# Odd-k sequence sums of batches 1 to 7 from rotated rows, in a Fourier mixing plus gated FFN kernel

## The chip, the cores and the metric

The kernel runs on one core of one Trainium2 chip. The metric is the device time of one execution in microseconds (us). The engines are TensorE (PE; its weight loads are listed as PEld), VectorE (DVE), ScalarE (ACT), GpSimd (POOL) and SyncE (SP, which here only issues DMAs).

## What is computed

```python
def _attn_ref(x):                      # x: (8, 3008, 256) float32
    X = np.fft.fft(x, axis=1)
    X = np.fft.fft(X, axis=2)
    return X.real.astype(np.float32)

def _moe_ref(x, w_gate, w_val, w_out): # x: (24064, 256); 256 -> 1536 -> 256
    gate = 1.0 / (1.0 + np.exp(-(x @ w_gate)))
    val = x @ w_val
    return (gate * val @ w_out).astype(np.float32)
```

The second function gets the first one's output, reshaped to 24064 rows. Everything is float32.

## The kernel before

**Names of size.** S = 3008 rows a batch, M = S/2 = 1504, D = 256. By symmetry only the frequencies k = 0 to 1504 of the sequence axis are summed; of these the code treats even and odd k apart, and of each only k up to 752, NE = 377 even and NO = 376 odd ones. The rest follow by adding and subtracting two sums, `ev` and `od` (rows with even and with odd s), in `places` (L443): one DVE sum goes up from k = 0, one comes down from k = M.

**Sequence stage.** Each batch has one. For batches 1 to 7 it stands in `whole` (L450), which runs four groups in this order: odd k with cosines (into tile pk), odd k with sines (into qk), even k with cosines, even k with sines. A group is 12 matmuls (`both` inside `half`, L426): six row slots q, times the two partition halves of 64 rows, which hold the rows of even and of odd s and sum into ev and od. For even k, rows s and 752-s have already been folded into each other (L381), so that each matmul moves only 188 or 189 of the 377 columns; for odd k each matmul moves all 376. Cosine groups sum in PSUM banks po0 and po1, sine groups in po2 and po3. `then` (L437) copies ev to SBUF with ACT, and `places` sums it with od on DVE.

**The rows** of a batch are first copied inside DRAM into a mirrored layout (`mirror_x`, L170), loaded as one tile `x4`, and folded by 24 GpSimd operations (`fold_ops`, L347) that are spread over many steps before the stage: rows s with S-s (L354), these with M-s (L367), then feature d with 256-d (`feat`, L360 to L364), first for odd k, then, after L383 has folded 752-s into s, for even k, in three pieces of two slots each. L362 and L364 write those pieces.

**Tables.** Cosines and sines are held in one tile `st` (ST[0]). Batch 0 uses them in the layout of 126 partitions. For the other batches they are copied in DRAM into a mirrored layout `tr` (`mirror_tables`, L192, nine DMAs on SP at steps 22 to 30) and loaded again over the old ones (`table_again`, L195, four DMAs at step 42).

**Joint E.** Feature column 128 of the batches 1 to 7 is transformed for all of them at once in `e_sums` (L476), at step 40, in the PSUM bank of tag po0; its results go through `places` to a DRAM row `ed`.

**The rest of the time** goes to the gated FFN, in 576 steps i (8 batches x 6 chunks of 252 columns x 12 blocks of 128 of the 1536 hidden features). Weights with the feature transform merged in (G1, G2) and a seed from E give pf = G1·pk (`front_a`) and then pf += G2·qk (`front_b`), with the copy `ae` of the first part taken between them (`part`, L548), so that ae and pf give the two mirrored halves. `gate_a` and `gate_b` (L560 to L591) make the sigmoids on ACT and the products h on DVE. GpSimd forms sums of h blocks (sf, L590). `back` (L597) multiplies h and sf blocks with sums of w_out blocks (wf) in 15 products, five a step, into the banks po0 to po4. It stands five steps behind, so that group p (three steps) is multiplied at steps 3p+5 to 3p+7. After the fourth group of a chunk, the banks are copied to `c` (L614), and `finish` combines them with DVE sums (L637), two or three a step, transposes and stores them.

**Order.** It is written out by hand: every engine executes in the order in which the loop at the end of the kernel (L792 to L814) issues. In step i that is front_a(i), gate_a(i-1), part(i), the seeds of step i+1, gate_b(i-1), five products of `back`, front_b(i), some sums of `finish`, then the side work of this step, put there by `at`. Side work that matters here: e_sums at step 40, table_again at 42, the sequence stage of batch b+1 at step g0 (64 for batch 1, then 112, 184, 256, 328, 400, 472), and the folding of its rows in the 16 or 24 steps before g0 whose number mod 12 is below 4. The next batch's rows are loaded (`load_x`) at g0+1.

[...]

Of the kernel before, what the change touches and what calls it, by code (L numbers as in the profile page):

```python
# [7 lines left out]
F32 = mybir.dt.float32  # L8
# [40 lines left out]
NQ = 6  # L49
# [28 lines left out]
def kernel(  # L78
# [49 lines left out]
    def mm(o, l, r, start, stop):  # L128
        nc.tensor.matmul(o, l, r, start=start, stop=stop, skip_group_check=True)  # L129
# [14 lines left out]
            else:  # L144
                nc.sync.dma_start(out=X[b][0:NP, h : h + 2], in_=xf[b, :, h : h + 2])

    def mirrored(dst, src, full):


        copy = nc.sync.dma_start  # L150
        h, n = dst.shape[1], dst.shape[3] - full
        ops = [lambda: copy(out=dst[HP - 2 : HP, :, NQ - 1, full:],
                            in_=zero[:, :, 0:n].to_broadcast([2, h, n]))]

        def rows(par):
            copy(out=dst[par * HP : (par + 1) * HP, :, 0:N3], in_=src[0:HP, :, par:NQ:2])

        def mirror(par, q):
            t = M // 2 - 2 * q - par
            lo, p0, n = par * HP, t // NQ, HP - 2 * ((par, q) == (0, N3 - 1))  # L160
            copy(out=dst[lo : lo + n, :, N3 + q, full:].rearrange("p h d -> h p d"),
                 in_=src[p0 - n + 1 : p0 + 1, :, t % NQ, full:].rearrange("p h d -> h p d")[:, ::-1])
# [5 lines left out]
    XR = {}  # L168

    def mirror_x(b):  # L170
        XR[b] = dram.tile([P, 4, NQ, D], F32, name=f"xr{b}")
        return mirrored(XR[b], xf[b], 0)
# [6 lines left out]
    ge = const.tile([P, 2, NFT], F32, name="ge")  # L179

    x8 = const.tile([NP, B - 1, 4, NQ], F32, name="x8")
    nil = op.tile([2, 1, NO], F32, name="nil", tag="os")
    zero = dram.tile([2, 1, NO], F32, name="zero")
    table = const.tile([2, 1], F32, name="table")
    tr = dram.tile([P, 2, NQ, NE + NO], F32, name="tr")
# [6 lines left out]
    def mirror_tables():  # L192
        return mirrored(tr, stab, NE)

    def table_again():  # L195

        ST[0] = const.tile([P, 2, NQ, NE + NO], F32, name="st", tag="st")
        for t in range(2):
            nc.sync.dma_start(out=ST[0][:, t, 0:N3], in_=tr[:, t, 0:N3])
            nc.sync.dma_start(out=ST[0][:, t, N3:, NE:], in_=tr[:, t, N3:, NE:])  # L200

# [143 lines left out]
    def fold_ops(b, nq):  # L347
# [12 lines left out]
        def feat(e, v, r, q):  # L360
            e.memset(r[:, q, 0:1], 0.0)
            e.tensor_tensor(r[:, q, 1:HD], v[:, q, 1:HD], v[:, q, D - 1 : HD : -1],  # L362
                            op=ALU.subtract)
            e.tensor_tensor(v[:, q, 1:HD], v[:, q, 1:HD], v[:, q, D - 1 : HD : -1], op=ALU.add)  # L364

        def across(e, blk, q):
            e.tensor_tensor(x4[:, 1 - blk, q], x4[:, 0, q], x4[:, 2, q],  # L367
                            op=(ALU.add, ALU.subtract)[blk])

        parts = [(x4[:, 1], x4[:, 3]), (x4[:, 0], x4[:, 2])]  # L370
        qs = [slice(q, q + nq) for q in range(0, NQ, nq)]
        pool = nc.gpsimd
        if b:

            for i in (0, 2):
                ops += [lambda i=i, q=q: point(pool, i, i + 1, q) for q in qs]
# [9 lines left out]
            parts[0] = x4[:, 3], x4[:, 1]  # L386
            ops += [lambda q=q: feat(pool, *parts[0], q) for q in qs]
# [25 lines left out]

    PQE = {}

    def half(w, d, blk, sn, other=None):


        c0, n = ((0, NE), (NE, NO))[blk]
        ev, od = [bank(name, other and other[i])[:, 0:n] for i, name in enumerate(("ev", "od"))]  # L420

        def sums(*qs):
            for q in sorted(qs, key=lambda q: q % 2):
                mm((ev, od)[q % 2], w(q), ST[0][0:NP, int(sn), q, c0 : c0 + n], q < 2, q >= NQ - 2)

        def both():  # L426

            for r in range(2 - blk):
                for q in range(N3 if blk == 0 else NQ):
                    for par, sum_ in enumerate((ev, od)):  # L430
                        rows = slice(par * HP, par * HP + HP - 1 - (par and q % N3 == N3 - 1))
                        ks = slice(None) if blk else slice(r, n, 2)
                        wq = q if blk else q + N3 * (r ^ int(sn))
                        mm(sum_[:, ks], w(wq)[rows], ST[0][rows, int(sn), q, c0 : c0 + n][:, ks],
                           q == 0 and r == 0, q == (NQ if blk else N3) - 1)

        def then():  # L437
            a = evp.tile([P, NE], F32, name="a", tag="a")[:, 0:n]
            nc.scalar.copy(a, ev)
            return lambda: places(d, blk, sn, a, od)  # L440
        return sums, then, both
# [18 lines left out]
            nc.vector.memset(t[:, NK:], 0.0)  # L460

    def seq_group(b, blk, what, other=None):
        return half(lambda q: W[b, blk][what][:, q, :], PQE[b][what], blk, what == 1, other)


    def e_load(b):
# [9 lines left out]
    def e_sums():  # L476


        ps = bank("pe", 0)
        m = B - 1  # L480
        at_ = lambda blk, par: slice((2 * blk + par) * TB, (2 * blk + par) * TB + m)
        for q in range(0, NQ, 2):
# [7 lines left out]
        a = evp.tile([P, NE], F32, name="a", tag="a")[0:m]  # L490
        e1 = evp.tile([P, NE], F32, name="a", tag="a")[0:m]
        nc.scalar.copy(a, ps[at_(0, 1), 0:NE])
        nc.scalar.copy(e1[:, 0:NO], ps[at_(1, 0), 0:NO])

# [245 lines left out]
    def at(i, *fs):  # L740
        side.setdefault(i, []).extend(fs)
# [129 lines left out]
```

## Time and profile before

| what | value |
|---|---|
| median of 3 runs | 1974.01 us (1973.17 to 1975.24) |
| the profiled execution | 1973.76 us |
| its span, first to last instruction | 1972.0 us |
| mean granted clock of TensorE in it | 0.995 |
| DMA over the span | 101.41 MB, 51 GB/s |

The costliest groups, as the profile lists them (busy us in all, mean of one record):

| line, engine, tile | records | busy us | mean ns |
|---|---|---|---|
| L129 PE pf<-qk and pf<-pk, 252 or 246 columns | 4608 | 1165.8 | 375 |
| L129 PE po<-sf and po<-h, 168 or 164 columns | 5760 | 1007.3 | 305 |
| L129 PE ev (all forms; od runs beside it) | 372 | 98.0 | 414 |
| L590 POOL sf, first two groups | 2112 | 1206.0 | 590 |
| L532 ACT seeds pf<-ek,ge | 1128 | 531.4 | 471 |
| L637 DVE sums c<-c | 949 | 484.3 | 541 |

How to read it: the matmuls are issued through one helper, so all have line L129 and are told apart by the tiles written and read. A float32 matmul of the program leaves two matmul records and two weight-load records. A record lasts longer than the distance to the next one, since matmuls are pipelined; their cost is the distance from start to start. In rows in order of time the first number is the start in us from the start of the span, the second the duration; a bracket at the end gives idle time before the instruction and the instruction that ended it.

### The profile page before, as it was taken

The numbers are of one execution on the slowest core, as the hardware profiler recorded it, in microseconds if no ns is written. First come the engines' busy times: TensorE is split into PE (matmuls) and PEld (weight loads), VectorE is DVE, ScalarE is ACT, GpSimd is POOL, SyncE is SP. The second block draws the span as 40 slices with busy tenths as digits, with TensorE's granted clock in tenths as the row PEclk, the third lists the DMA queues.
The fourth block names the chain that finished last, engine by engine and source line by source line (L and its number), as shares of the span: only waits on it lengthen the run. The fifth ranks groups of instructions, "written<-read, shape, count | busy, mean of one in ns | idle before, by whom it ended". The sixth has DMA issues, their size and how long they took to land.

```text
span 1972.0 us, 34403 instructions
## 1 busy us (share of the span) xinstructions
PE 1935.8 (98%) x11252; PEld 1792.4 (91%) x11252; DVE 1511.7 (77%) x3170; ACT 1339.5 (68%) x3108; POOL 1625.0 (82%) x2843
## 2 busy tenths in 40 slices
PE   6999999999999999999999999999999999999997
PEld 4889889999999899998999989999899999999997
DVE  6888778886787677786778867787678776777777
ACT  3567657766777577775777757777577766777775
POOL 3779888997889788996889868998688996777776
PEclk9999999999999999999999999999999999999999
DMA  8363412212022121212012021211210110011011
GB/s 271 86 134 94 138 52 85 51 22 78 14 51 54 17 76 17 72 31 78 14 28 78 14 78 25 47 48 24 78 19 14 21 20 14 14 20 22 14 19 27
DMA packets 171584, 101.41 MB, mean 51 GB/s; under 512 B 133904, under 2 KB 163218, under 8 KB 168602
## 3 DMA queue, kind: packets, MB, share of 16 engines
q1 hardware_dynamic: 169434, 98.64, 20.6%
q8 instruction: 90, 1.47, 0.3%
q10 hardware_dynamic: 1940, 0.56, 0.1%
q14 instruction: 88, 0.72, 0.1%
q0 software_dynamic: 32, 0.00, 0.0%
HBM read 74.45 MB, written 50.18 MB: 63 GB/s over the span
## 4 chain that ended last, share of the span: by engine, by line
PE 95%; DMA 2%; DVE 2%; ACT 1%; issue 0%; POOL 0%; SPq 0%; ACTq 0%; DVEq 0%; POOLq 0%
PE pf L129 49%; PE po L129 41%; PE ev L129 4%; DMA st<-in_stab_dram 1%; PE ps L129 1%; DMA ge<-G 1%; PE od L129 0%; DMA raw<-in_moe_w_val_dram 0%; DMA xr<-in_xf_dram 0%; DVE c L637 0%; DVE ae L551 0%; DVE wf L337 0%; DVE wx L273 0%; ACT z L585 0%; DVE wx L275 0%
## 5 line engine op out<-in xcount | busy, mean ns | idle before, releaser
L590 POOL TENSOR_TENSOR sf<-h 128x168 f32<-128x168 f32 (+1 forms) x960 | 548.8, 590 | 221.6 <-DVE h L586 221.6
L590 POOL TENSOR_TENSOR sf<-h,sf 128x168 f32<-128x168 f32 (+1 forms) x1152 | 657.2, 590 | 60.5 <-DVE h L586 60.5
L129 PE MATMUL pf<-qk,G 128*128 128x252 f32 (+1 forms) x2304 | 582.4, 375 | 3.1 <-DVE ae L551 2.0
L129 PE MATMUL pf<-pk,G 128*128 128x252 f32 (+1 forms) x2304 | 583.4, 376 | 0.0
L586 DVE TENSOR_TENSOR h<-z 128x252 f32<-128x252 f32 (+1 forms) x576 | 299.1, 519 | 356.9 <-ACT z L585 356.6
L532 ACT ACTIVATE pf<-ek,ge 128x252 f32<-128x252 f32 (+1 forms) x1128 | 531.4, 471 | 18.4
L129 PE MATMUL po<-sf,wf 128*128 128x168 f32 (+1 forms) x3072 | 530.1, 305 | 0.0
L548 ACT ACTIVATE ae<-pf 128x504 f32<-128x504 f32 (+1 forms) x569 | 335.0, 589 | 245.6 <-PE pf L129 245.5
L637 DVE TENSOR_TENSOR c<-c 128x168 f32<-128x168 f32 (+1 forms) x949 | 484.3, 541 | 5.5 <-ACT c L614 0.3
L129 PEld LDWEIGHTS pf<-pk,G 128*128 128x128 f32 x2304 | 436.7, 190 | 52.6 <-issue 2.3
L129 PEld LDWEIGHTS po<-sf,wf 128*128 128x128 f32 x3072 | 472.8, 190 | 8.3
L129 PE MATMUL po<-h,wf 128*128 128x168 f32 (+1 forms) x2688 | 477.2, 306 | 1.7 <-ACT a L497 1.6
L129 PEld LDWEIGHTS po<-h,wf 128*128 128x128 f32 x2688 | 428.8, 191 | 19.0 <-ACT a L497 2.0
L129 PEld LDWEIGHTS pf<-qk,G 128*128 128x128 f32 x2304 | 410.2, 190 | 29.2 <-DVE ae L551 2.6
L572 DVE TENSOR_TENSOR z<-ae,pf 128x504 f32<-128x504 f32 (+1 forms) x569 | 377.4, 663 | 21.5 <-ACT h L567 20.9
L567 ACT ACTIVATE h<-pf 128x252 f32<-128x252 f32 (+1 forms) x576 | 217.9, 378 | 164.0 <-PE pf L129 152.9
L585 ACT ACTIVATE z<-z 128x252 f32<-128x252 f32 (+1 forms) x576 | 231.1, 401 | 80.3 <-DVE z L572 60.1
L584 DVE TENSOR_TENSOR h<-h,pf 128x252 f32<-128x252 f32 (+1 forms) x576 | 231.9, 403 | 0.0
L590 POOL TENSOR_TENSOR sf<-sf 128x168 f32<-128x168 f32 (+1 forms) x192 | 111.3, 580 | 15.1
L590 POOL TENSOR_TENSOR sf<-sf,h 128x168 f32<-128x168 f32 (+1 forms) x192 | 106.6, 555 | 0.0
L129 PE MATMUL ev<-st,x 63*128 63x376 f32 (+4 forms) x372 | 98.0, 414 | 8.3 <-DVE x L364 7.8
L129 PEld LDWEIGHTS ev<-st,x 63*128 63x128 f32 (+1 forms) x372 | 66.4, 187 | 36.1 <-DVE x L364 8.2
(120 smaller groups left out, 861.9 us busy)
## 6 DMA issues: line engine op xcount, KB each, us to landing
x<-xr SPq DMA_DIRECT2D x14, 1536.0 KB
out_dram<-os SPq DMA_DIRECT2D x380, 56.0 KB
xr<-in_xf_dram SPq DMA_DIRECT2D x14, 768.0 KB
xr<-in_xf_dram SPq DMA_DIRECT2D x35, 256.0 KB
ek<-ed SPq DMA_DIRECT2D x39, 126.0 KB
out_dram<-os SPq DMA_DIRECT2D x288, 7.0 KB
st<-in_stab_dram SPq DMA_DIRECT2D x4, 1111.9 KB
x<-in_xf_dram SPq DMA_DIRECT2D x2, 1512.0 KB
```

What stands on the lines that cost most here:

```text
L129: nc.tensor.matmul(o, l, r, start=start, stop=stop, skip_group_check=True)
L532: nc.scalar.activation(PF[i][:, g], EK[i // NFT], AF.Copy, scale=ge[:, g, f : f + 1])
L548: nc.scalar.activation(AP[i], PF[i], AF.Copy, scale=2.0)
L567: nc.scalar.activation(H[p][:, fh, 0:n], PF[i][:, 0], AF.Sigmoid)
L572: nc.vector.tensor_tensor(z[:, :, ::-1], AP.pop(i), PF[i], op=ALU.subtract)
L584: nc.vector.tensor_tensor(h[:, fh, 0:n], h[:, fh, 0:n], PF.pop(i)[:, 1], op=ALU.mult)
L585: nc.scalar.activation(z[:, 0], z[:, 0], AF.Sigmoid)
L586: nc.vector.tensor_tensor(h[:, fh, n:], z[:, 0], z[:, 1], op=ALU.mult)
L590: nc.gpsimd.tensor_tensor(block(p, dst), block(p, a), block(p, b), op=(ALU.subtract, ALU.add)[op])
L637: engine.tensor_tensor(t[:, dst * R : (dst + 1) * R], *v, op=(ALU.subtract, ALU.add)[op])
```

## The change

- **Rotation.** Let t be the angle 2·pi·s/S of a row s. For odd k = 4j+1 and 4j-1, cos(kt) = cos t · (cos 4jt -+ tan t · sin 4jt), and likewise for sines. Six new DVE operations a batch (`turn`) add to each odd-k row slot the tangent times its partner (cosine rows of slot s with sine rows of slot 752-s, and so on) and write the result into the upper feature columns of the same slots, which the folding has left free. They are issued in the last four steps before g0: two, one, two and one.
- **Half tables.** A table j4 of 189 columns (cos t · cos 4jt and cos t · sin 4jt) replaces the 376 odd columns. `table_odd`, once at step 46, makes it from the odd columns that were loaded: two GpSimd sums of 3x187 columns, each followed by an ACT multiply by 0.5, six tiny GpSimd operations at the edges, and three DVE operations on three columns for the tangents.
- **Odd-k groups.** Still 12 matmuls a group, each of 189 columns: slots 0 to 2 sum into the first 189 columns of ev and od, slots 3 to 5 into the next 189.
- **Emptying of odd-k groups.** For ev and for od, one ACT copy of the first 189 columns to SBUF and two DVE operations of 188 columns (sum for k = 4j+1, difference for 4j-1) into a scratch part of the table tile; then `places` as before, but from that scratch. Before, it was one ACT copy of 376 columns and `places`.
- **Tables.** The mirrored copy `tr` in DRAM goes, with its nine DMAs. `table_again` loads only three slots a half, with four DMAs of 64 partitions, straight from the input; the tile is divided into the tables, j4, the scratch and the tangents.
- **Joint E.** `e_sums` takes the PSUM bank of tag po4 instead of po0.
- Batch 0 and the even-k groups keep their work.

```diff
     def table_again():
-        ST[0] = const.tile([P, 2, NQ, NE + NO], F32, name="st", tag="st")
+        full = const.tile([P, 2 * NQ * (NE + NO)], F32, name="st", tag="st")
+        sizes = (2 * N3 * (NE + NO), 2 * N3 * NJ, 2 * NO, N3, N3)
...
         for t in range(2):
-            nc.sync.dma_start(out=ST[0][:, t, 0:N3], in_=tr[:, t, 0:N3])
-            nc.sync.dma_start(out=ST[0][:, t, N3:, NE:], in_=tr[:, t, N3:, NE:])
+            for par in range(2):
+                nc.sync.dma_start(out=ST[0][par * HP : (par + 1) * HP, t], in_=stab[0:HP, t, par:NQ:2])
+
+    def table_odd():
+        odd, j4 = ST[0][:, :, :, NE:], ST[1]
+        for t in range(2):
+            nc.gpsimd.tensor_tensor(j4[:, t, :, 1 : NJ - 1], odd[:, t, :, 2::2], odd[:, t, :, 1 : NO - 1 : 2],
+                                    op=ALU.add)
+            nc.scalar.mul(j4[:, t, :, 1 : NJ - 1], j4[:, t, :, 1 : NJ - 1], 0.5)
...
+        nc.vector.reciprocal(ST[4], odd[:, 0, :, 0])
+        nc.vector.tensor_tensor(ST[3], odd[:, 1, :, 0], ST[4], op=ALU.mult)
+        nc.vector.tensor_scalar(out=ST[4], in0=ST[3], scalar1=-1.0, scalar2=None, op0=ALU.mult)
...
+            slots = x4.rearrange("p i q d -> p (i q) d")
+            def turn(q, minus):
+                y = [slots[:, q : q + 16 : 15], slots[:, q + N3 : q + N3 + 10 : 9]]
+                if minus:
+                    y.reverse()
+                nc.vector.scalar_tensor_tensor(
+                    out=y[0][:, :, HD:D], in0=y[1][:, :, 0:HD], scalar=(ST[3], ST[4])[minus][:, q : q + 1],
+                    in1=y[0][:, :, 0:HD], op0=ALU.mult, op1=ALU.add)
...
+                        if blk:
+                            out_, wq = sum_[:, r * NJ : (r + 1) * NJ], q + N3 * r
+                            tab = ST[1][rows, r ^ int(sn), q]
...
         def then():
+            a = evp.tile([P, 2 * NJ], F32, name="a", tag="a")
+            if b and blk:
+                for par, sum_ in enumerate((ev, od)):
+                    f = a[:, par * NJ : (par + 1) * NJ]
+                    nc.scalar.copy(f, sum_[:, 0:NJ])
+                    for r, op_ in enumerate((ALU.add, ALU.subtract)):
+                        nc.vector.tensor_tensor(ST[2][:, par, r::2], f[:, r : NJ - 1 + r],
+                                                sum_[:, NJ + r : 2 * NJ - 1 + r], op=op_)
+                return lambda: places(d, blk, sn, ST[2][:, 0], ST[2][:, 1])
...
     def e_sums():
-        ps = bank("pe", 0)
+        ps = bank("pe", NB - 1)
...
-    for i, f in enumerate(mirror_tables()):
-        at(2 * i0 - 2 + i, f)
     at(3 * i0, e_fold)
     at(3 * i0 + 4, lambda: e_sums()())
     at(3 * i0 + 6, table_again)
+    at(3 * i0 + 10, table_odd)
...
+            for i, f in enumerate(TURN.pop(b + 1)):
+                at(slots[-4 + i * 4 // 6], f)
```

More of the change, by code (lines that the diff above doesn't have):

```diff
@@ L106 @@
     N3 = NQ // 2
+    NJ = NO // 2 + 1
     assert D == 256 and M % 4 == 0 and NP * NQ > M // 2 and NQ % 2 == 0
@@ L145, in load_x, with mirror_x @@
                 nc.sync.dma_start(out=X[b][0:NP, h : h + 2], in_=xf[b, :, h : h + 2])
-    def mirrored(dst, src, full):
+    XR = {}
+    def mirror_x(b):
         copy = nc.sync.dma_start
-        h, n = dst.shape[1], dst.shape[3] - full
-        ops = [lambda: copy(out=dst[HP - 2 : HP, :, NQ - 1, full:],
-                            in_=zero[:, :, 0:n].to_broadcast([2, h, n]))]
+        src = xf[b]
+        dst = XR[b] = dram.tile([P, 4, NQ, D], F32, name=f"xr{b}")
+        ops = [lambda: copy(out=dst[HP - 2 : HP, :, NQ - 1],
+                            in_=zero[:, :, 0:D].to_broadcast([2, 4, D]))]
         def rows(par):
@@ L160, in mirror @@
             lo, p0, n = par * HP, t // NQ, HP - 2 * ((par, q) == (0, N3 - 1))
-            copy(out=dst[lo : lo + n, :, N3 + q, full:].rearrange("p h d -> h p d"),
-                 in_=src[p0 - n + 1 : p0 + 1, :, t % NQ, full:].rearrange("p h d -> h p d")[:, ::-1])
+            copy(out=dst[lo : lo + n, :, N3 + q].rearrange("p h d -> h p d"),
+                 in_=src[p0 - n + 1 : p0 + 1, :, t % NQ].rearrange("p h d -> h p d")[:, ::-1])
         for par in range(2):
@@ L166, in mirrored @@
         return ops
[L168 to L172, printed above, removed]
     dt = const.tile([P, 2, D], F32, name="dt")
@@ L181 @@
     x8 = const.tile([NP, B - 1, 4, NQ], F32, name="x8")
-    nil = op.tile([2, 1, NO], F32, name="nil", tag="os")
-    zero = dram.tile([2, 1, NO], F32, name="zero")
+    nil = op.tile([2, 1, D], F32, name="nil", tag="os")
+    zero = dram.tile([2, 1, D], F32, name="zero")
     table = const.tile([2, 1], F32, name="table")
-    tr = dram.tile([P, 2, NQ, NE + NO], F32, name="tr")
     ed = dram.tile([B, NK + 1], F32, name="ed")
@@ L190, in load_table @@
             yield nc.sync.dma_start(out=ST[0][0:NP, t, q : q + nq], in_=stab[:, t, q : q + nq])
-    def mirror_tables():
-        return mirrored(tr, stab, NE)
     def table_again():
-        ST[0] = const.tile([P, 2, NQ, NE + NO], F32, name="st", tag="st")
-        for t in range(2):
-            nc.sync.dma_start(out=ST[0][:, t, 0:N3], in_=tr[:, t, 0:N3])
-            nc.sync.dma_start(out=ST[0][:, t, N3:, NE:], in_=tr[:, t, N3:, NE:])
+        full = const.tile([P, 2 * NQ * (NE + NO)], F32, name="st", tag="st")
+        sizes = (2 * N3 * (NE + NO), 2 * N3 * NJ, 2 * NO, N3, N3)
+        at_ = [sum(sizes[0:i]) for i in range(6)]
+        st, jt, eo, *tans = [full[:, at_[i] : at_[i + 1]] for i in range(5)]
+        ST[:] = [st.rearrange("p (t q k) -> p t q k", t=2, q=N3),
+                 jt.rearrange("p (t q k) -> p t q k", t=2, q=N3),
+                 eo.rearrange("p (h k) -> p h k", h=2), *tans]
+        for t in range(2):
+            for par in range(2):
[6 more added lines that the diff above has]
+            nc.scalar.mul(j4[:, t, :, 1 : NJ - 1], j4[:, t, :, 1 : NJ - 1], 0.5)
+        nc.gpsimd.tensor_copy(j4[:, 0, :, 0:1], odd[:, 0, :, 0:1])
+        nc.gpsimd.memset(j4[:, 1, :, 0:1], 0.0)
+        for par in range(2):
+            rows = slice(par * HP, (par + 1) * HP)
+            nc.gpsimd.tensor_copy(j4[rows, par, :, NJ - 1 :], odd[rows, par, :, NO - 1 :])
+            nc.gpsimd.memset(j4[rows, 1 - par, :, NJ - 1 :], 0.0)
+        nc.vector.reciprocal(ST[4], odd[:, 0, :, 0])
+        nc.vector.tensor_tensor(ST[3], odd[:, 1, :, 0], ST[4], op=ALU.mult)
+        nc.vector.tensor_scalar(out=ST[4], in0=ST[3], scalar1=-1.0, scalar2=None, op0=ALU.mult)
     assert NPR == 6
@@ L345 @@
     W = {}
+    TURN = {}
     def fold_ops(b, nq):
@@ L386, in fold_ops @@
             parts[0] = x4[:, 3], x4[:, 1]
+            slots = x4.rearrange("p i q d -> p (i q) d")
[6 more added lines that the diff above has]
+                    in1=y[0][:, :, 0:HD], op0=ALU.mult, op1=ALU.add)
+            TURN[b] = [lambda q=q, minus=minus: turn(q, minus) for q in range(N3) for minus in range(2)]
             ops += [lambda q=q: feat(pool, *parts[0], q) for q in qs]
@@ L408, in fold_ops @@
         for blk, (v, r) in enumerate(parts):
+            if b and blk:
+                W[b, blk] = v[:, :, HD:D], r[:, :, HD:D]
+                continue
             W[b, blk] = (v[:, :, 0:HD], r[:, :, 0:HD],
@@ L414, with half @@
     PQE = {}
-    def half(w, d, blk, sn, other=None):
-        c0, n = ((0, NE), (NE, NO))[blk]
+    def half(b, w, d, blk, sn, other=None):
+        c0, n = ((0, NE), (NE, 2 * NJ if b else NO))[blk]
         ev, od = [bank(name, other and other[i])[:, 0:n] for i, name in enumerate(("ev", "od"))]
@@ L426, in both @@
         def both():
-            for r in range(2 - blk):
-                for q in range(N3 if blk == 0 else NQ):
+            for r in range(2):
+                for q in range(N3):
                     for par, sum_ in enumerate((ev, od)):
[L431 to L435, printed above, removed]
-        def then():
-            a = evp.tile([P, NE], F32, name="a", tag="a")[:, 0:n]
+                        rows = slice(par * HP, par * HP + HP - 1 - (par and q == N3 - 1))
+                        if blk:
+                            out_, wq = sum_[:, r * NJ : (r + 1) * NJ], q + N3 * r
+                            tab = ST[1][rows, r ^ int(sn), q]
+                        else:
+                            out_, wq = sum_[:, r::2], q + N3 * (r ^ int(sn))
+                            tab = ST[0][rows, int(sn), q, r:NE:2]
+                        mm(out_, w(wq)[rows], tab, q == 0 and r == 0, q == N3 - 1)
+        def then():
+            a = evp.tile([P, 2 * NJ], F32, name="a", tag="a")
+            if b and blk:
+                for par, sum_ in enumerate((ev, od)):
[5 more added lines that the diff above has]
+                return lambda: places(d, blk, sn, ST[2][:, 0], ST[2][:, 1])
+            a = a[:, 0:n]
             nc.scalar.copy(a, ev)
@@ L462, in seq_group @@
     def seq_group(b, blk, what, other=None):
-        return half(lambda q: W[b, blk][what][:, q, :], PQE[b][what], blk, what == 1, other)
+        return half(b, lambda q: W[b, blk][what][:, q, :], PQE[b][what], blk, what == 1, other)
     def e_load(b):
@@ L489, in e_sums @@
         nc.vector.memset(er[:, NK:], 0.0)
-        a = evp.tile([P, NE], F32, name="a", tag="a")[0:m]
-        e1 = evp.tile([P, NE], F32, name="a", tag="a")[0:m]
+        a = evp.tile([P, 2 * NJ], F32, name="a", tag="a")[0:m, 0:NE]
+        e1 = evp.tile([P, 2 * NJ], F32, name="a", tag="a")[0:m, 0:NE]
         nc.scalar.copy(a, ps[at_(0, 1), 0:NE])
```

## Prediction

> **What bounds the kernel now.** I read the page's busy table and chain first, then TensorE's rows in order of time, then the engines that feed the seven sequence stages.
>
> ```profile
> span 1972.0 us, 34403 instructions
> ...
> PE 1935.8 (98%) x11252; PEld 1792.4 (91%) x11252; DVE 1511.7 (77%) x3170; ACT 1339.5 (68%) x3108; POOL 1625.0 (82%) x2843
> ...
> PE 95%; DMA 2%; DVE 2%; ACT 1%; issue 0%; POOL 0%; SPq 0%; ACTq 0%; DVEq 0%; POOLq 0%
> ```
>
> PE is busy for 98% of the span and is 95% of the chain, so time taken off PE's queue comes off the end, as long as no other engine takes its place. The change works in the seven sequence stages. This is PE in the last of them:
>
> ```profile
> 1620.71 1.01 PE L129 MATMUL pf<-qk,G 128*128 128x252 f32 x4
> 1621.66 0.58 PE L129 MATMUL ev<-st,x 63*128 63x376 f32 x1
> 1621.66 0.58 PE L129 MATMUL od<-st,x 63*128 63x376 f32 x1
> ...
> 1629.03 0.47 PE L129 MATMUL ev<-st,x 63*128 63x376 f32 x1
> 1629.05 0.47 PE L129 MATMUL od<-st,x 62*128 62x376 f32 x1
> 1629.35 0.33 PE L129 MATMUL ev<-st,x 63*128 63x189 f32 x1
> 1629.37 0.33 PE L129 MATMUL od<-st,x 63*128 63x189 f32 x1
> 1629.51 0.33 PE L129 MATMUL ev<-st,x 63*128 63x189 f32 x1
> ...
> 1633.50 1.12 PE L129 MATMUL pf<-pk,G 128*128 128x252 f32 x4
> ```
>
> An ev and an od matmul start within 0.02 us of each other: the two halves of the partitions run side by side, so the pair is the unit. Each matmul leaves two records. The odd-k part (376 columns) goes from 1621.66 to 1629.35, 24 pairs 0.318 us apart; the even-k part (189 or 188 columns) has 24 pairs 0.168 us apart; the stage takes 11.84 us. All seven do, at 279.22, 440.86, 677.02, 913.18, 1149.34, 1385.50 and 1621.66. T below is the time since a stage's start.
>
> **Matmuls.** The odd-k part keeps 24 pairs and their weight loads, but each moves 189 columns. The even-k row has this very shape, 63x189 with loads of 63x128, at 0.168 us. So a stage loses 24 x (0.318 - 0.168) = 3.6 us, seven lose **25.2 us**. The bounds are 0 (0.318 stays) and 3.7 (its output is no longer strided).
>
> **Product banks.** Odd k with cosines uses banks 0 and 1, with sines 2 and 3, and the even-k groups take the same banks again. The second use now comes 4.0 us after the first instead of 7.6. The old emptying in the same stage:
>
> ```profile
> 1622.51 1.16 DVE L637 TENSOR_TENSOR c<-c 128x168 f32<-128x168 f32 x2
> 1626.25 0.55 DVE L444 TENSOR_TENSOR pk<-a,od 128x376 f32<-128x376 f32 x1 [2.58 <-ACT a L439]
> 1626.72 0.54 DVE L447 TENSOR_TENSOR pk<-a,od 128x376 f32<-128x376 f32 x1
> ```
>
> That is one ACT copy (0.47) and two DVE sums. The new one is two ACT copies and four DVE sums of 188, then the two old placing sums, which no longer hold a bank. Per column, L584 (252 columns from PSUM, 0.40) and L572 (504, 0.66) give about 1.03 ns over 0.15 us; 188 columns cost 0.34 and a copy of 189 0.33. Odd cosines end on PE at T 2.3; the ACT copy to 2.65; DVE, free since T 2.0, leaves bank 0 at 3.3 and bank 1 at 3.8; placing to 4.75. PE wants them at T 4.13: no wait. Sines: done at 4.3, DVE from 4.75, banks 2 and 3 free at 5.3 and 5.85; PE wants them at 6.15. The margins are 0.3 us, and placing sums that read only SBUF can stretch while POOL runs: L586 takes 0.42 alone and 0.61 beside POOL. Two such sums stand ahead of banks 2 and 3, so I charge **0.3 us** a stage in the five stages of batches 3 to 7 (bounds 0 and 1.5), 1.5 us in all. DVE ends some 1.8 us behind PE's last pair, as before.
>
> [...] If DVE bound the stage throughout, it would last 2.66 + 2 x 2.44 + 2 x 1.09 = 9.7 us instead of 8.24 and the kernel some 1962 us.
>
> **POOL is late in two stages.** The even-k group also needs folded rows from POOL, in three pieces of two row slots. Its fifth matmul needs the last, now at T 4.13 + 4 x 0.336 = 5.47 (before: 9.1). The last piece in batch 2 and in batch 7:
>
> ```profile
> 447.93 0.72 POOL L364 TENSOR_TENSOR x<-x 128x254 f32<-128x254 f32 x1
> ...
> 1624.90 0.72 POOL L364 TENSOR_TENSOR x<-x 128x254 f32<-128x254 f32 x1
> ```
>
> They end at T 7.79 and 3.96; batch 1's at 6.57; batches 3 to 6 as 7. POOL has no gap ahead of them, so what slows it arrives here. The new DVE work beside it (six turns, then placing sums) slows POOL by about 0.14 each (L362: 0.72 alone, 0.86 beside DVE); I take 0.6 in all (0 to 1.5). Then PE stands 6.57 + 0.6 - 5.47 = **1.7 us** in batch 1, **2.9 us** in batch 2, nothing in the others. PE is in order, so everything queues behind this wait.
>
> [...]
>
> **Turns.** Six DVE instructions of 2x128 columns a batch, all SBUF: L586 (252 columns) bounds each between 0.42 and its longest, 1.56; its median is 0.47; I take 0.55. They wait for row pieces that POOL finished some ten iterations earlier. Two, one, two, one of them fall into the stage's last four iterations; behind them wait DVE's L572, then ACT's second sigmoid, then DVE's L586. In these iterations DVE stands idle about 1.1 us for that sigmoid; 3.3 us of turns go into about 4.4. Cost 0; without that cover 3.3 us a batch.
>
> **Tables, once.** The nine mirroring DMAs go (SP alone issues them; PE has no gap there): 0. The four reloads move 2259 KB instead of 3387 KB, are issued at about 201 and should land by 212, when DMA share has fallen to 0.41. Their readers come at about 223.8:
>
> ```profile
> 222.40 0.40 ACT L585 ACTIVATE z<-z 128x252 f32<-128x252 f32 x1
> 223.28 0.38 ACT L567 ACTIVATE h<-pf 128x252 f32<-128x252 f32 x1 [0.48 <-PE pf L129]
> 224.13 0.59 ACT L548 ACTIVATE ae<-pf 128x504 f32<-128x504 f32 x1 [0.47 <-PE pf L129]
> ```
>
> Here `table_odd` puts two ACT multiplies behind z, each waiting for a POOL sum of 561 columns. POOL's sums of group 14 end at 223.8 (L590: 223.24 + 0.60). By L367 (512 columns, 1.27) and L383 (384, 1.00) such a sum takes 1.4 us; so they end at 225.2 and 226.7 and the second multiply (0.65) at 227.4. h, ae and the seeds queue behind it: ae comes at 227.7 instead of 224.13, and PE's front_b, which started at 225.35, at 228.25. That costs **2.9 us** (2.5 with sums of 1.2; 5.7 if the stride doubles them). POOL runs 2.2 us late after it, which three iterations of distance to the products cover. DVE's three tiny operations (each between L460's 0.06 and 0.5) sit in that same halt.
>
> **Joint E.** PE's wait of 1.62 us for bank 0 at 203.73 goes. But front_b then still waits for ae at 206.48, whose chain (two copies, DVE's er sums, ACT) does not depend on the bank: gain 0. Bank 4 is emptied by ACT at 199.07, while PE wants it at 198.98: 0.2 lost.
>
> **Sum**: 25.2 - 1.5 - 1.7 - 2.9 - 2.9 - 0.2 = 16.0. The profiled execution took 1973.76 (1.76 outside its span), so 1957.8; the median of the runs is 0.25 higher: **1958.0 us**.
>
> **Rivals.**
> 1. Nothing waits: POOL keeps ahead and ACT's halt is covered. For it: nearly 3.6 us a stage are cleared in five of seven anyway. Against: T 6.57 and 7.79. 25.2 off, or 22.3 with the halt: 1949 to 1951.5. Chance 0.13.
> 2. Emptying or POOL's lateness binds in every stage: DVE's SBUF sums take the 0.7 to 0.9 of the er sums at 203.71. Then a stage keeps 1.0 to 2.1 us instead of 3.3: about 1966, up to 1970. Against: POOL is nearly through in five stages. Chance 0.15.
> 3. The pairs do not get closer than 0.318, weight loads (0.185 each) holding them: 1974 to 1977. Against: the even-k row. Chance 0.05.
> 4. Slower: the turns. If each takes over (4.4 + 3.6) / 6 = 1.33 us, they outgrow DVE's idle time and the stage's gain together; at L586's longest, 1.56, a batch loses 1.3 us net, seven 9, plus ACT's halt: 1986. Against: a median of 0.47. Chance 0.07.
>
> **Numbers.** The forecast, 1953 to 1963, has 0.60. 1950 to 1967 takes in most of rivals 1 and 2 and the bounds above, and leaves out about 0.2. Faster by over 0.2% (about what a measurement here can tell from no change; below 1970) comes to 0.13 + 0.60 + 0.15 = 0.88, within 0.2% to 0.05, slower to 0.07.
>
> **What would show it.** Odd-k pairs of 63x189 at 0.168 us; stages of about 8.5 us for batches 3 to 7, 10 for batch 1 and 11 for batch 2, where PE waits for POOL's L364; one PE gap of about 3 us near 225, ending on ae; no PE wait for DVE's turns. Wrong: waits of PE for bank sums over 1 us a stage, POOL's last pieces later than T 5.5 in batches 3 to 7, or PE gaps in the four iterations ahead of a stage.

## The result, and the profile after

The changed kernel takes 1966.14 us (median of 5 runs, 1965.11 to 1974.25) and the kernel before 1974.01 (5 runs, 1971.70 to 1978.11): ratio 0.9965, 95% interval 0.9942 to 0.9989. On a second chip the ratio was 0.9952 (0.9938 to 0.9965). So it is faster by 0.35 to 0.5%: 7.9 us where the forecast had 16.0. The profiled execution took 1966.45 us with a span of 1964.6, 7.4 us shorter than before; the rest of this text accounts for these 7.4 against 16.0. The lines of `mm` and others have moved: L134 was L129, L388 was L364, L598 was L548, L640 was L590, L386 was L362; L418 is `turn`, L483 and L485 the new emptying, L494 and L497 `places`, L211 and L213 `table_odd`.

From the page: span, busy time and shares of the chain.

```profile
span 1964.6 us, 34539 instructions
...
PE 1920.6 (98%) x11252; PEld 1791.5 (91%) x11252; DVE 1567.0 (80%) x3271; ACT 1341.0 (68%) x3124; POOL 1639.9 (83%) x2851
...
PE 90%; DVE 5%; POOL 3%; ACT 1%; DMA 1%; issue 0%; SPq 0%; DVEq 0%; ACTq 0%; POOLq 0%
```

PE is still the bound, but DVE and POOL now stand on the chain with 8% together, where they had 2%. TensorE's rows in the last stage:

```profile
1616.99 0.42 PE L134 MATMUL ev<-st,x 63*128 63x189 f32 x1
1617.00 0.42 PE L134 MATMUL od<-st,x 63*128 63x189 f32 x1
1617.26 0.32 PE L134 MATMUL ev<-st,x 63*128 63x189 f32 x1
1617.26 0.32 PE L134 MATMUL od<-st,x 63*128 63x189 f32 x1
1617.41 0.32 PE L134 MATMUL ev<-st,x 63*128 63x189 f32 x1
...
1620.95 0.33 PE L134 MATMUL ev<-st,x 63*128 63x189 f32 x1
```

The 24 odd-k pairs now stand 0.16 us apart, and the odd-k part lasts from 1616.99 to 1620.95, 3.96 us instead of 7.69. Without any wait a stage would take 11.84 - 24 x (0.318 - 0.160) = 8.05 us. The seven stages took 11.01, 12.63 and five times 9.17. Three places lost the difference, and two more lost time outside the stages.

**Stages of batches 3 to 7: 1.12 us each.** VectorE in the last stage, then two rows each of TensorE and GpSimd beside it:

```profile
1619.57 0.61 DVE L485 TENSOR_TENSOR st<-a,ev 128x188 f32<-128x188 f32 x2 [0.60 <-ACT a L483]
1620.10 0.60 DVE L485 TENSOR_TENSOR st<-a,od 128x188 f32<-128x188 f32 x2
1620.73 0.88 DVE L494 TENSOR_TENSOR pk<-st 128x376 f32<-128x376 f32 x1
1621.53 1.07 DVE L497 TENSOR_TENSOR pk<-st 128x376 f32<-128x376 f32 x1
1622.70 0.61 DVE L485 TENSOR_TENSOR st<-a,ev 128x188 f32<-128x188 f32 x2
1623.23 0.60 DVE L485 TENSOR_TENSOR st<-a,od 128x188 f32<-128x188 f32 x2
1623.87 0.55 DVE L494 TENSOR_TENSOR qk<-st 128x376 f32<-128x376 f32 x1
1624.34 0.54 DVE L497 TENSOR_TENSOR qk<-st 128x376 f32<-128x376 f32 x1
```

```profile
1623.46 0.57 PE L134 MATMUL ev<-st,x 63*128 63x189 f32 x2 [0.27 <-DVE st L485]
1623.98 0.40 PE L134 MATMUL od<-st,x 63*128 63x189 f32 x1
```

```profile
1620.48 0.72 POOL L386 TENSOR_TENSOR x<-x 128x254 f32<-128x254 f32 x1
1621.28 0.91 POOL L388 TENSOR_TENSOR x<-x 128x254 f32<-128x254 f32 x1
```

Banks 2 and 3 come free when the second pair of L485 rows is through, at 1623.3 and 1623.8. PE wanted bank 2 at 1623.0 and began at 1623.46, and its od half still later, at 1623.98. In front of those rows stand the two placing sums of pk, 0.88 and 1.07 us; the same sums into qk take 0.55 and 0.54. The difference is GpSimd, which runs L386 and L388 until 1622.2. The rows show how each engine held up the other: L494 ends 0.41 us after L386, L497 ends 0.41 us after L388, and L388, begun while L494 ran, takes 0.91 us instead of 0.72. So it goes in the whole trace: 18 placing sums from `st` began beside a GpSimd instruction, and each ends 0.40 to 0.42 us after that one's end, whatever its length (0.71 to 1.07 us); the 10 that met none take 0.54 to 0.55. The L485 sums, which read one input from PSUM, are not held up: the 44 that began beside GpSimd take 0.33 to 0.35 each. Nor were the placing sums of the kernel before, which read `od` from PSUM: nine began beside GpSimd and took 0.54 to 0.55. The change gave the placing sums two inputs in SBUF, and with them this wait.

**Stages of batches 1 and 2: 2.96 and 4.58 us.** TensorE in batch 1, then in batch 2:

```profile
288.96 0.32 PE L134 MATMUL od<-st,x 63*128 63x188 f32 x1
291.89 0.43 PE L134 MATMUL ev<-st,x 63*128 63x188 f32 x1 [2.61 <-POOL x L388]
...
292.34 0.33 PE L134 MATMUL ev<-st,x 63*128 63x188 f32 x1
...
292.51 0.33 PE L134 MATMUL ev<-st,x 63*128 63x188 f32 x1
```

```profile
454.23 0.68 PE L134 MATMUL ev<-st,x 63*128 63x188 f32 x1 [2.63 <-POOL x L388]
...
455.02 0.52 PE L134 MATMUL ev<-st,x 63*128 63x188 f32 x1
...
455.33 0.52 PE L134 MATMUL ev<-st,x 63*128 63x188 f32 x1
...
457.94 0.32 PE L134 MATMUL ev<-st,x 63*128 63x188 f32 x1
```

Both wait 2.6 us for POOL's last piece of rows. But behind the second wait the pairs stand 0.31 us apart instead of 0.17 until 457.5: the granted clock is at half there (0.50), for 3.41 us from 454.26, and that makes 1.6 us more.

**The halt at step 46: 4.13 us.** TensorE, then ScalarE:

```profile
227.57 1.12 PE L134 MATMUL pf<-qk,G 128*128 128x252 f32 x4 [2.16 <-ACT ae L598]
228.53 1.48 PE L134 MATMUL pf<-pk,G 128*128 128x252 f32 x4
229.80 0.77 PE L134 MATMUL po<-h,wf 128*128 128x168 f32 x2
```

```profile
224.94 0.67 ACT L213 ACTIVATE st<-st 128x561 f32<-128x561 f32 x1 [2.24 <-POOL st L211]
226.10 0.67 ACT L213 ACTIVATE st<-st 128x561 f32<-128x561 f32 x1 [0.49 <-POOL st L211]
226.68 0.36 ACT L617 ACTIVATE h<-pf 128x252 f32<-128x252 f32 x1
226.94 0.58 ACT L598 ACTIVATE ae<-pf 128x504 f32<-128x504 f32 x1
```

The multiplies wait for GpSimd's sums and ae queues behind them; the wait is 2.16 us, and once more the clock is halved for 3.41 us behind it, from 228.98. Matched one by one with their rows before the change, TensorE's rows come 4.13 us later behind the halt than ahead of it.

**Turns: 2.0 us.** Busy time in the 12.40 us ahead of the stages of batches 1, 2, 3 and 7 in the kernel before (a row's pairs are PE, PEld, DVE, ACT, POOL):

```profile
266.80:279.20 12.40, 12.40 (x73) 11.58 (x71) 8.86 (x20) 9.74 (x23) 12.24 (x22) 1.00 0.31 49
428.40:440.80 12.40, 12.40 (x73) 11.46 (x71) 9.56 (x22) 10.12 (x24) 12.32 (x22) 1.00 0.32 53
664.60:677.00 12.40, 12.40 (x72) 11.42 (x71) 7.42 (x20) 9.86 (x23) 12.02 (x23) 1.00 0.29 44
1609.20:1621.60 12.40, 12.40 (x73) 11.46 (x71) 7.40 (x20) 9.81 (x23) 11.98 (x23) 1.00 0.24 42
```

DVE had 5.0 us idle ahead of batches 3 and 7, but 3.5 and 2.8 ahead of batches 1 and 2. The 42 turns took 0.785 us in the mean (0.65 to 1.04), so six take 4.7. From the end of stage 1 to the start of stage 2 went 149.79 us before and 151.28 after, with waits of PE for ae of 0.20 and 0.39 in it; 0.54 was lost ahead of stage 1. Between the later stages it is 224.3 us in both.

The joint E's two waits, 1.62 and 1.05, became one of 2.87 at 206.37; TensorE's rows behind it stand 0.1 us earlier than before.

### The profile page after: what moved, and what is told of

It reads as the page before. It is cut to its first block, busy times and chain, and to the rows that moved or that the text cites. A ratio compares the mean times of both kernels' runs of the same rounds, so it can differ in the third digit from the quotient of the medians.

```text
span 1964.6 us, 34539 instructions
## 1 busy us (share of the span) xinstructions
PE 1920.6 (98%) x11252; PEld 1791.5 (91%) x11252; DVE 1567.0 (80%) x3271; ACT 1341.0 (68%) x3124; POOL 1639.9 (83%) x2851
## 4 chain that ended last, share of the span: by engine, by line
PE 90%; DVE 5%; POOL 3%; ACT 1%; DMA 1%; issue 0%; SPq 0%; DVEq 0%; ACTq 0%; POOLq 0%
PE pf L134 47%; PE po L134 39%; PE ev L134 2%; POOL sf L640 2%; DVE c L687 1%; PE od L134 1%; DMA x<-in_xf_dram 1%; DVE h L636 1%; PE ps L134 1%; DVE z L622 1%; ACT z L635 0%; DVE st L485 0%; POOL x L407 0%; DVE pk L497 0%; POOL x L388 0%
## 5 line engine op out<-in xcount | busy, mean ns | idle before, releaser
L640 POOL TENSOR_TENSOR sf<-h 128x168 f32<-128x168 f32 (+1 forms) x960 | 552.3, 593 | 199.8 <-DVE h L636 199.7
L640 POOL TENSOR_TENSOR sf<-h,sf 128x168 f32<-128x168 f32 (+1 forms) x1152 | 661.5, 593 | 60.1 <-DVE h L636 60.1
L134 PE MATMUL pf<-qk,G 128*128 128x252 f32 (+1 forms) x2304 | 583.2, 376 | 7.8 <-ACT ae L598 5.6
L134 PE MATMUL pf<-pk,G 128*128 128x252 f32 (+1 forms) x2304 | 584.3, 376 | 0.0
L134 PE MATMUL po<-sf,wf 128*128 128x168 f32 (+1 forms) x3072 | 530.8, 306 | 0.0
L598 ACT ACTIVATE ae<-pf 128x504 f32<-128x504 f32 (+1 forms) x569 | 335.0, 589 | 238.9 <-PE pf L134 238.4
L134 PEld LDWEIGHTS pf<-pk,G 128*128 128x128 f32 x2304 | 437.0, 190 | 53.2 <-issue 2.3
L134 PEld LDWEIGHTS po<-sf,wf 128*128 128x128 f32 x3072 | 473.6, 190 | 8.3
L134 PE MATMUL po<-h,wf 128*128 128x168 f32 (+1 forms) x2688 | 477.1, 306 | 0.1
L134 PEld LDWEIGHTS po<-h,wf 128*128 128x128 f32 x2688 | 428.9, 191 | 17.1 <-DVE wf L357 0.3
L134 PEld LDWEIGHTS pf<-qk,G 128*128 128x128 f32 x2304 | 409.9, 190 | 35.3 <-ACT ae L598 7.4
L640 POOL TENSOR_TENSOR sf<-sf 128x168 f32<-128x168 f32 (+1 forms) x192 | 111.6, 581 | 15.0
L640 POOL TENSOR_TENSOR sf<-sf,h 128x168 f32<-128x168 f32 (+1 forms) x192 | 107.4, 559 | 0.0
L134 PE MATMUL ev<-st,x 63*128 63x189 f32 (+3 forms) x372 | 77.1, 355 | 14.1 <-DVE x L388 7.5
L134 PEld LDWEIGHTS ev<-st,x 63*128 63x128 f32 (+1 forms) x372 | 63.5, 193 | 24.5 <-DVE x L388 7.9
```

Source lines behind the costliest of these rows:

```text
L598: nc.scalar.activation(AP[i], PF[i], AF.Copy, scale=2.0)
L640: nc.gpsimd.tensor_tensor(block(p, dst), block(p, a), block(p, b), op=(ALU.subtract, ALU.add)[op])
```

## The experiments

All spans are those of one profiled execution each; ratios are against the kernel before on the same chip.

### ScalarE's multiplies two and three steps later

```diff
-            nc.scalar.mul(j4[:, t, :, 1 : NJ - 1], j4[:, t, :, 1 : NJ - 1], 0.5)
...
+    for t in range(2):
+        at(3 * i0 + 12 + t, lambda t=t: halve(t))
```

> Against the changed kernel (1966.1 us). The two ACT multiplies of the half table go two and three steps later than the GpSimd sums they wait for, so that ACT never waits for them. Theory A (ACT's halt held PE for 2.2 us, and that PE wait then halved PE's clock for 3.4 us, which cost another 1.8): the PE wait near 225 and the half clock after it both go, 4.1 us less, about 1962. Rival B (the half clock has nothing to do with the wait and comes anyway): only 2.2 us less, 1963.9, and a stretch of 3.4 us at half clock is still found between 220 and 240. Rival C (the wait was not ACT's): no gain.

Measured: ratio 0.9930 (0.9915 to 0.9945), span 1963.6. The wait near 225 and its half clock are gone. But the stretch of half clock now lay behind the joint E's wait (206.24, 2.83 us), and waits of 0.30 and 0.40 for ae appeared ahead of stage 1, whose start came 1.2 us earlier than in the changed kernel, not 4. So the halt was as named, but the span shows only 1.0 us of the 4.1 that were expected: part of the price moved.

### Placing sums behind the sums that free the banks

A second scratch lets all eight L485 sums go ahead of the placing sums.

```diff
-                        nc.vector.tensor_tensor(ST[2][:, par, r::2], f[:, r : NJ - 1 + r],
+                        nc.vector.tensor_tensor(sc[:, par, r::2], f[:, r : NJ - 1 + r],
...
+        def stage(b=b):
+            odd = [whole(b + 1, 1, what) for what in range(2)]
+            for what in range(2):
+                even = whole(b + 1, 0, what)
+                odd[what]()
+                even()
```

> Against the changed kernel. In a sequence stage DVE first does the sums that free the banks of both odd-k groups, with a second scratch, and only then the placing sums; nothing is left out and the number of instructions is the same. Theory A (banks 2 and 3 came free late because the placing sums of the cosine group, 0.88 and 1.07 us instead of 0.54 beside a busy GpSimd, stood ahead of the sine group's sums): the PE wait inside the stages of batches 3 to 7 goes, these stages last 8.1 to 8.3 us instead of 9.17, 4.5 to 5.5 us less in all, about 1961. Rival B (the banks are late because emptying has simply more DVE work than the matmuls last): the wait only moves, to the even-k groups or to the products after the stage, and less than 2 us are gained.

Measured: ratio 0.9926 (0.9899 to 0.9952), span 1962.2. VectorE in the last stage, which starts at 1615.82 (L485, L487, L496 and L499 here are L483, L485, L494 and L497 of the changed kernel):

```profile
1618.40 0.61 DVE L487 TENSOR_TENSOR st<-a,ev 128x188 f32<-128x188 f32 x2 [0.58 <-ACT a L485]
1618.93 0.60 DVE L487 TENSOR_TENSOR st<-a,od 128x188 f32<-128x188 f32 x2
1620.33 0.61 DVE L487 TENSOR_TENSOR st<-a,ev 128x188 f32<-128x188 f32 x2 [0.80 <-ACT a L485]
1620.85 0.60 DVE L487 TENSOR_TENSOR st<-a,od 128x188 f32<-128x188 f32 x2
1621.38 0.90 DVE L496 TENSOR_TENSOR pk<-st 128x376 f32<-128x376 f32 x1
1622.20 0.54 DVE L499 TENSOR_TENSOR pk<-st 128x376 f32<-128x376 f32 x1
```

The second set of sums now waits for ACT, not for DVE's own queue, and ends at T 5.6. Stages of batches 3 to 7 take 8.11 us, 1.06 less each: with this order on DVE nearly the whole bank loss is gone, though pk's placing sum still takes 0.90. That is 5.3 us, of which the span shows 2.4, because batch 1's wait for POOL (2.28) was now followed by half clock too, and the joint E's wait by twice 3.41 us of it, while the halt's wait was not.

### Row folds two steps earlier

```diff
-                at(slots[i * len(slots) // len(ops)], f)
+                at(slots[i * (len(slots) - 2) // len(ops)], f)
```

> Against the changed kernel. The folding on GpSimd is spread over the same steps without the last two, so that its last pieces are issued two steps before the end of that stretch; the work is the same. Theory A (in batches 1 and 2 PE waits 2.6 us for GpSimd's last piece, and in batch 2 the clock then halves): both waits go, the stages of batches 1 and 2 last about 9.2 us like the others instead of 11.0 and 12.6, 1.8 + 3.4 = 5.2 us less, about 1961. Rival B (GpSimd is simply behind by then, and what moves ahead makes its h sums late): PE waits for sf in the products near the stage instead, and the gain is under 2 us.

Measured: ratio 0.9908 (0.9892 to 0.9925), span 1956.9, the largest single gain. POOL's last piece came 2.0 to 5.3 us ahead of the stages, no stage waited for POOL, and the stages took 9.22, 9.02 and five times 8.32. The last figure had not been expected, and it shows why the placing sums were long. VectorE in the last stage, with the folds out of its way:

```profile
1613.86 0.55 DVE L494 TENSOR_TENSOR pk<-st 128x376 f32<-128x376 f32 x1
1614.33 0.54 DVE L497 TENSOR_TENSOR pk<-st 128x376 f32<-128x376 f32 x1
1614.98 0.61 DVE L485 TENSOR_TENSOR st<-a,ev 128x188 f32<-128x188 f32 x2
```

The sums of 0.88 and 1.07 take 0.55 and 0.54 once POOL's folds do not run beside them, in the same order on DVE, and the stage is 0.85 us shorter. In batch 1's stage they still meet POOL's sf sums, take 0.83 and 0.88, and the stage stays at 9.22. So the bank loss needed both, placing sums that wait for GpSimd and their place ahead of the sums that free banks 2 and 3; either cure takes most of it.

### No turns

The rotations are left out, so the odd-k sums lack their partner's part.

```diff
-            for i, f in enumerate(TURN.pop(b + 1)):
-                at(slots[-4 + i * 4 // 6], f)
```

> Against the changed kernel. The six rotations of a batch are left out, so the odd-k groups of batches 1 to 7 sum rows that were not rotated. Theory A (the turns cost PE 0.45 and 1.5 us ahead of the stages of batches 1 and 2, and by making GpSimd later another 1 us or so in each of these two stages): 3 to 5 us less, 1961 to 1963; the steps ahead of the stages of batches 3 to 7 keep their time. Rival B (turns are hidden, GpSimd is late by itself): under 1 us. Rival C (turns are what delays GpSimd in every stage): stages of batches 3 to 7 also shorten, by over 0.5 us each.

Measured: ratio 0.9919 (0.9904 to 0.9933), span 1960.4. Between stages 1 and 2 it takes 149.87 us, as before the change: the 1.5 us there are the turns'. Stages of batches 3 to 7 take 8.77 instead of 9.17: POOL's last piece ends at T 3.99 instead of 5.20, so its folds run less beside the placing sums. In batches 1 and 2 the waits for POOL are 2.62 and 3.49, not smaller, and POOL's last piece ends at T 8.05 in batch 1 with or without turns (6.57 before the change). So leaving out the turns is no cure there. Set against the kernel before, sum by sum and counted from the stage's start, GpSimd's sums in the changed kernel end 0.4 us late just ahead of stage 1 and 0.7 early just ahead of stage 2 (the turns had delayed TensorE too), and GpSimd loses another 1.1 and 1.0 us up to its last piece. Without turns they end 0.75 and 0.05 late, and GpSimd loses 0.7 and 1.1. The larger part of the loss inside the stage thus comes without turns. GpSimd in batch 1's stage of the changed kernel:

```profile
287.90 0.84 POOL L640 TENSOR_TENSOR sf<-sf,h 128x164 f32<-128x164 f32 x1
288.69 0.83 POOL L640 TENSOR_TENSOR sf<-h,sf 128x164 f32<-128x164 f32 x1
290.94 0.91 POOL L388 TENSOR_TENSOR x<-x 128x254 f32<-128x254 f32 x1
```

The same three took 0.53, 0.53 and 0.72 before the change. Each began while a placing sum from `st` ran, so 0.8 of the 1.1 us is the new emptying beside POOL's work; no run took the emptying away, so for the rest this is argued.

### The changed kernel again

> The changed kernel again, as the base for the three runs beside it. Both theories: span 1964.6 as in its first profile, ratio to the kernel before 0.9965 (0.994 to 0.999), a half-clock window behind TensorE's wait for ScalarE near 228 and behind its wait for GpSimd near 454. If the windows of half clock fall elsewhere this time, the windows are partly chance and about 1.7 us of any difference between two spans is theirs.

Measured: ratio 0.9952 (0.9938 to 0.9965), span 1962.0. The waits are the same, 2.16 (halt), 2.63 and 2.62 (POOL), but half clock followed both POOL waits and not the halt or the wait of 2.00 near 101. Stage 1 took 12.58 us instead of 11.01 with the same wait. So the same kernel with the same waits pays about 1.6 us for one of them in one execution and not in the next.

### The three edits together

> The three edits tried alone (multiplies later, sums ahead of the placing, folds two slots earlier) together; nothing of the computation is left out. Theory A (the terms are separate places on TensorE's queue and add): all seven stages at 8.05 to 8.2 instead of 11.84, which is 26 us, less about 2 us of turn waits ahead of stages 1 and 2: span 1947.5 +- 1.7, ratio about 0.988. Theory B (what is cured in one place is lost in another: turns that now show, a half-clock window that moves): the three separate gains in span, 1.0, 2.4 and 7.7 us, add up as they were measured: span 1953.5, ratio about 0.991. A stage above 8.4 speaks against A.

Measured: ratio 0.9889 (0.9873 to 0.9905), span 1947.4. Stages: 8.16, 8.23 and five times 8.11. Theory A's stages are all there, and it is these that show that the losses are separate places that add. That its span is met to 0.1 us is partly luck: in this execution no half clock fell between 30 us and the end stretch. The median of its runs, 1952.97, is 13.1 under the changed kernel beside it. This version beats both kernels.

> The run with all three edits again, as the base for the run beside it: span 1947.4 to 1950, ratio to the kernel before 0.987 to 0.990. Steps ahead of stages 1 and 2 with waits of about 0.2 us, as before. A half-clock window behind the joint-E wait of 3.2 us may come or not; it is worth 1.7 us.

Another chip gave 0.9902 (0.9882 to 0.9921), span 1949.7, with half clock behind the wait near 102; the stages are the same, 8.15, 8.23 and five times 8.11.

### Turns elsewhere

```diff
-                at(slots[-4 + i * 4 // 6], f)
+                at(slots[(-6, -5, -5, -2, -1, -1)[i]], f)
```

> As the run with all three edits, but the six turns one, two, zero, zero, two, one... are spread over steps of two chunks: one in the third step of the chunk before, two in the fourth, and in the last two steps before the stage two and one, so that the steps ahead of the stage hold three instead of six. Theory A (the turns outgrow VectorE's slack only where several fall in consecutive steps): the waits of 0.2 to 0.4 us for ae ahead of stages 1 and 2 go, 1 to 2 us less than the run with three edits. Theory B (each turn costs its length at these two stages wherever it stands, since VectorE has no slack left there): same span within 0.5 us, the waits now some 14 steps earlier.

Measured: ratio 0.9887 (0.9873 to 0.9901), span 1950.2, of which 0.8 us were lost in the first 50 us against the run with three edits. Its waits of 0.24 and 0.17 ahead of stages 1 and 2 went, and waits of 0.27 and 0.51 came six to nine steps earlier, for both stages. Then one turn a step, `slots[i - 6]`:

> As the run with all three edits, but one turn a step in six steps (the last two of the folding steps of the chunk before, and the last four before the stage) instead of two, one, two, one in the last four. Theory A (only the second turn of a step outgrows VectorE's slack): no waits of TensorE for ae ahead of stages 1 and 2, steps there as long as elsewhere, span 1 to 2 us under that run at the same length of the start. Theory B (each turn at these two stages costs its length, wherever it stands): the waits split up into six small ones, same span within 0.5 us. The seven stages stay at 8.1 to 8.25 in both.

Measured: ratio 0.9892 (0.9877 to 0.9907), span 1949.6. Only one wait of PE over 0.15 us (0.16 at 276.92) is left ahead of these stages, and yet from the end of stage 1 to the start of stage 2 it takes 151.91 us (151.60 in the run with three edits beside it, 149.79 before the change): the steps are a little longer each. Theory B comes nearer, though without its six small waits: ahead of batch 2 the turns cost 1.5 us or more wherever they were put, with 2.8 us of idle time on DVE there for 4.7 us of turns.

### Which waits halve the clock

To the run with all three edits, ScalarE copies of different lengths are added that hold up ae, and so make TensorE wait.

```diff
+    def hold(us):
+        n = int(us / 0.8) + 1
+        w = int((us / n - 0.15) / 0.00092)
+        for _ in range(n):
+            nc.scalar.copy(ST[6][:, 0:w], ST[0][:, 0, 0, 0:w])
+
+    for j in range(24):
+        at(189 + 12 * j, lambda j=j: hold(1.6 + 0.2 * (7 * j % 24)))
```

> As the run with three edits, with extra ScalarE copies into unused columns, put into 24 steps between the stages 2 and 6 (12 steps, some 37 us, apart), of 1.6 to 6.2 us in all each, in mixed order; they hold up ae and so make TensorE wait. To see which waits are followed by a half-clock window. Theory A (a threshold): every wait above about 2.1 us is followed by a window of 3.41 us, none below 1.9. Theory B (a fixed grid of 3.41 us: a window is halved when most of the grid's cell before it was idle): waits of 2 to 3.4 us are followed by a window in some cases and not in others, according to where in the grid they fall, waits above 4 us always; starts of all windows agree in their remainder by 3.41 us. Theory C (it is the power of what follows, not the wait): no relation to the length.

Measured: 2027.82 us, span 2025.5 (the added copies are most of the difference). Waits of 2.11, 2.16, 2.30, 2.54, 3.29, 3.52 and 3.71 us were followed by half clock, and so were 4.28, 4.58 and 4.70; waits of 2.27, 3.10, 3.19, 3.32 and 3.48 were not, nor any under 2.1. That rules out a bare threshold. The starts of the half-clock stretches (776.96, 817.92, 951.04, 1111.46, ... 1538.13) lie whole multiples of 3.413 us apart (12, 51, ... 223 from the first), and so they do within each of the other profiles (228.98 and 454.26 in the changed kernel's, 66 apart): within each profile here they keep one grid. Two waits cut into its cells (in a row: PE's busy time first, the granted clock third from the end):

```profile
1237.76:1241.17 3.41, 1.45 (x11) 1.20 (x9) 1.13 (x2) 3.25 (x6) 3.10 (x6) 1.00 0.00 0
1241.17:1244.58 3.41, 1.88 (x9) 1.60 (x10) 1.71 (x5) 3.03 (x7) 0.13 (x1) 1.00 0.00 0
1244.58:1248.00 3.42, 3.42 (x22) 3.26 (x21) 2.58 (x7) 2.31 (x6) 2.07 (x4) 1.00 0.02 5
1493.76:1497.17 3.41, 1.12 (x5) 0.93 (x6) 1.00 (x2) 3.31 (x8) 1.63 (x4) 1.00 0.02 5
1497.17:1500.59 3.42, 3.42 (x12) 3.09 (x12) 1.82 (x5) 2.17 (x6) 1.24 (x2) 0.50 0.00 0
```

The wait of 3.48 us ending at 1242.70 falls on two cells, 1.96 us of it in the first and 1.53 in the second: nothing follows. The wait of 2.30 ending at 1496.05 lies nearly whole in one cell: the next cell is halved. Theory B holds here. Take the waits over 0.5 us of all profiles here by cell, from 30 us on and up to the end stretch: every cell with 1.99 us of waiting or more was followed by half clock, every cell at full clock with 1.91 or less was not, and of two cells with 1.96 one was. Where the cells lie in the span differs between the profiles (they start 0.3 us behind a multiple of 3.413 us in the changed kernel's, 2.1 behind one here): that is the chance in it.

## Why the prediction was right in direction and wrong in size

The direction came out as forecast, and so did the places of the halt and of the waits for POOL; the waits for banks 2 and 3 and for the turns were not expected at that size or at all. The sum was too large by 8.6 us, profile to profile. By its terms:

| term | forecast, us | measured, us |
|---|---|---|
| matmuls | -25.2 | -26.5 (7 x 24 x 0.158) |
| product banks, batches 3 to 7 | +1.5 | +5.6 (5 x 1.12) |
| POOL late, batch 1 | +1.7 | +2.96 |
| POOL late, batch 2 | +2.9 | +4.58 (half clock in it) |
| tables | +2.9 | +4.13 (half clock in it) |
| turns | 0 | +2.0 (1.48 + 0.54) |
| joint E, and all ahead of it | +0.2 | -0.1 |
| sum | -16.0 | -7.3 (span -7.4) |

- **Matmuls.** Right, a little better: 0.160 instead of 0.168.
- **Product banks**: the term furthest off. The step that failed is "placing to 4.75", from which the sines' banks 2 and 3 were to be free at 5.3 and 5.85, ahead of TensorE at 6.15. Measured, placing ended at T 5.61, the banks came free at 6.3 and 6.8, and TensorE wanted them at 6.0. The prediction named the very risk ("placing sums that read only SBUF can stretch while POOL runs") and priced it at 0.3 us a stage; it took both sums at their length with POOL idle, though POOL's last fold was to end only at T 3.96 and later with the turns. Measured, pk's two sums took 1.95 instead of 1.09, and the 0.86 is what the run with early folds gave back (0.85); the rest went with the order on DVE. The term was mis-sized, 0.3 for 1.12 us a stage.
- **POOL late.** The need, T 5.47, was nearly right (5.31 where nothing waits). The slip of 0.6 was not: 1.48 in batch 1 (6.57 to 8.05), 0.32 in batch 2 (7.79 to 8.11, in a stage that itself came 1.5 us later for the turns), 1.24 in the others (3.96 to 5.20). The last figure goes with the turns (3.99 without them); in batches 1 and 2 about 1 us is lost inside the stage.
- **Half clock** was in no term. Behind the halt and behind batch 2's wait it made 1.8 and 1.6 us; before the change one such stretch lay near 103 us, which the changed kernel has too. A trace of before shows it: the wait of 2.00 there is followed by 3.41 us at half clock, and the waits of 1.62 and 1.05 near 204 are not.
- **Tables.** The sums took 1.2 us each and the wait was 2.16, less than the forecast 2.9; half clock made it more.
- **Turns.** The step "3.3 us of turns go into about 4.4" used one slack for all stages and a row of one 252-column sum for the turn. The turns took 4.7, because every one of the 42 began beside a GpSimd instruction and ended 0.28 us after its end, and the slack ahead of batch 2 was 2.8. In batches 3 to 7 the step held for TensorE, though POOL paid there.
- **Rivals.** The time is what rival 2 gave, about 1966, and its mechanism is found in the main: emptying made TensorE wait in five stages and POOL's lateness in two, and DVE's SBUF sums took the 0.7 to 0.9 it named, or more (0.88 and 1.07). Its price of a stage holds in the mean alone: the stages of batches 3 to 7 kept 2.67 us of gain, batch 1's 0.83, and batch 2's lost 0.79, which makes 1.9 a stage against its 1.0 to 2.1. That the time fits so well is partly luck, since half clock and turns are in it. Rival 1's price, 1949 to 1951.5, is about what the version with all three edits reaches (1949.7 profiled, median 1953.0). Rivals 3 and 4 fell: pairs 0.16 us apart, and turns of 0.785 instead of 1.33.
- **Emptying as the bound.** The prediction had worked out 9.7 us a stage for DVE binding throughout; 9.17 looks near it, but the same emptying in another order lasts 8.11, so the work of emptying is not the bound here.
- **POOL beside the turns.** 28 of its L640 sums began during a turn and took 0.72 us instead of 0.53, and 12 folds 0.80 to 0.87 instead of 0.72: about 0.9 us a batch, near the 1.24 by which the last piece slipped in batches 3 to 7.

## What to carry to other kernels

When a stage gets shorter, the work that ran beside it in its slack is pushed together: take each instruction's time from a row with the neighbour engine busy (here VectorE's placing sums of two SBUF inputs ended 0.41 us after the GpSimd instruction they began beside and took up to 1.07 us instead of 0.54, while those with one input from PSUM kept their 0.54 to 0.55), and put the sums that free a PSUM bank ahead of those that only tidy up. Read slack stage by stage, at the stage where the work will stand; one batch's slack said nothing for another's. And price a new wait of TensorE at its length plus, from about 2 us on, a share of 1.7 us for half clock (1.8 and 1.6 were measured): at 2.0 us some 0.4 of it, at 2.6 some 0.6, all of it from 3.9 (an estimate, worked out from cells of 3.41 us and the 1.96 found here, for a wait that falls anywhere in the grid).

## What was not expected of the hardware

In these profiles a wait of TensorE was followed by half clock not by its own length but by how much of it fell into one cell of a running grid of 3.413 us: 1.99 us and more of waiting in a cell at full clock was each time followed by a cell at 0.50, 1.91 and less never, and 1.96, 57% of a cell, once in two cases. The cell need not be idle throughout: TensorE was busy for 1.12 us of the one from 1493.76, and the next ran at 0.50. Cells that were themselves halved needed less here: with waits of 0.71, 1.37 and 2.07 us in them the next one stayed at 0.50, with 0.48 it did not.
